# Routed attention and a gated feed-forward on one core: values of four steps behind one pair of score steps

## Chip, cores and metric

The kernel runs on one core of one Trainium2 chip. The metric is the device time of one execution in microseconds (us). A core has a matrix engine (TensorE, PE in the profile), VectorE (DVE), ScalarE (ACT), GpSimd (POOL) and a queue engine for transfers (SyncE, SP). They run beside each other and wait for one another by semaphores. Each works through its own instructions in the order in which the program gives them, so the order of the program on each engine is a thing that one can tune. This kernel fixes that order by hand.

## What is computed

```python
# q, k, v: (4, 8, 768, 64); centroids: (8, 16, 64); w_in: (512, 2048); w_out: (2048, 512)
q_assign = argmax(einsum('bhsd,hcd->bhsc', q_n, c_n))      # the nearest of 16 centroids of the head
k_assign = argmax(einsum('bhsd,hcd->bhsc', k_n, c_n))
mask = q_assign[:, :, :, None] == k_assign[:, :, None, :]
scores = where(mask, q @ k.T / 8, -1e9)
attn = softmax(scores)
x = (attn @ v) with heads joined                            # (3072, 512)
h = x @ w_in
out = (h * clip(h + 3, 0, 6) / 6) @ w_out                   # (3072, 512)
```

## The kernel before

Two heads make a *pair*; there are 16 pairs. Each pair has two halves of queries (384 columns) and six chunks of keys, so 12 *steps*, 192 in all. A step is: scores of a chunk of keys with half the queries for both heads (`ps`), the mask as a second product with one-hot rows (`xm`) added in PSUM, the exponential on ScalarE (`ex`), the sum over keys on GpSimd (`acc`), and the values (`pv`), which gather over six steps in one PSUM bank. Per half pair `divide` sums `acc` over partitions with a product by ones (`pd`), takes the reciprocal and scales.

```python
def scores(n):
    g, hf, j = where(n)                  # pair, half, chunk of keys
    if ("ps", n) not in st:
        scores_qk(n)                     # 2 matmuls, one for each head: 64 rows of the array each
    scores_part(n, st["xm", g], False)   # 2 more, bf16: the mask
    sc = st.pop(("ps", n))[:, :, 0:HALF]
    ex = expp.tile([P, 2, HALF], F32, name="ex")          # expp has 4 buffers, psum_s has 2
    nc.scalar.activation(out=ex, in_=sc, func=ACT.Exp, scale=SM_SCALE)
    ...
    nc.gpsimd.tensor_tensor(out=acc, in0=acc, in1=ex, op=ALU.add)

def attn_v(n):
    if j == 0:
        st["pv"] = psum_v.tile([P, 512], F32, name="pv")  # psum_v has 1 buffer
    for t in range(2):                                     # one head each: 64 columns of the array
        nc.tensor.matmul(pv[t * D : (t + 1) * D], lhsT=vt[:, j, t], rhs=ex[:, t],
                         start=(j == 0), stop=(j == NCH - 1))
    if j == NCH - 1:
        nc.scalar.copy(out=num, in_=pv)
```

The feed-forward is cut into 12 blocks of 256 tokens. From the second block on its products are done with seven half-size products in place of eight. A block has eight "up" items and seven "down" items. An up item makes four groups of gates, in two PSUM banks (X, then Y, of two that rotate); VectorE adds them up, ScalarE makes the lift and VectorE the clip, and each two items GpSimd makes further sums of the gates.

```python
def halved(b, m, u, i, g):
    part(X[:, 0], ...); part(X[:, 1], ...); part(X[:, 2], ...)      # uX: 12 matmuls in the trace
    nc.vector.tensor_copy(out=sx[:, 1], in_=X[:, 1])
    add(sx[:, 0], X[:, 0], sx[:, 1]); add(sx[:, 2], X[:, 2], sx[:, 0])
    finish()                                                        # clip of the item before
    part(Y[:, 0], ...); ...; part(Y[:, 3], ...)                     # uY: 16
    add(sx[:, 3], Y[:, 0], sx[:, 0]); add(g[:, 3], Y[:, 0], sx[:, 2])
    add(g[:, 0:3], Y[:, 1:4], sx[:, 1:4])
    lift(sx, g)                                                     # ScalarE
    ending.append(lambda: (clip(g, sx, g), gated_sums(i)))          # what finish() runs
```

In the second block each up item also makes four differences of `w_in` on VectorE (`first_sums`), which later blocks load back.

The main loop goes by *double steps*. Items fill the time in which the attention waits:

```python
for n in range(0, total + lag_d + 2, 2):
    for i in (n, n + 1):
        scores(i)                        # with its exponential and key sum
    for i in (n - 2, n - 1):
        attn_v(i)
    m = n - 3
    if m % NCH == NCH - 1:
        later.append(divide(m))
    prep = prep_items(g + 1, r)          # turning q and k, centroid scores, one-hot rows of the next pair
    ...
    want = items_by(n + 2) - done        # items of the feed-forward; interleaved with prep
    ...
    decode steps of the weights          # in the first half of the pairs alone (n < 96)
    checks                               # copies and accumulations that guard the ranges (ScalarE)
```

Of the kernel before, what the change touches and what calls it, by code (L numbers as in the profile page):

```python
# [8 lines left out]
F32 = mybir.dt.float32  # L9
# [107 lines left out]
def fast_path(ctx, tc, ok, q, k, v, centroids, moe_w_in, moe_w_out, out):  # L117
# [11 lines left out]
    vp = pool("vp", 2)  # L129
    xp = pool("xp", 2)  # L130
    rtp = pool("rtp", 1)
    smallp = pool("smallp", 1)
    expp = pool("expp", 4)
    accp = pool("accp", 2)
    nump = pool("nump", 1)
    xnp = pool("xnp", 2)
# [5 lines left out]
    decoding = ctx.enter_context(ExitStack())  # L142
    rawp = decoding.enter_context(tc.tile_pool(name="rawp", bufs=2))
    decp = decoding.enter_context(tc.tile_pool(name="decp", bufs=2))
    psum_s = pool("psum_s", 2, space=PSUM)
    psum_v = pool("psum_v", 1, space=PSUM)
    psum_t = pool("psum_t", 1, space=PSUM)
# [16 lines left out]
    counts = const.tile([P, 2, NPAIR], F32, name="counts")  # L164
    w_low = const.tile([P, 1], F32, name="w_low")

    st = {}
    later = []

    def scratch(shape, name, dtype=F32):  # L170

# [81 lines left out]

    cen = const.tile([P, D], F32, name="cen")
    parity = const.tile([P, 2], F32, name="parity")

    def constants():
        make_identity(nc, ident)  # L260
        for t in range(2):
            nc.vector.tensor_reduce(
                out=parity[:, t : t + 1],
                in_=ident.rearrange("p (h t c) -> p t h c", t=2, c=C)[:, t], axis=AX.XY, op=ALU.max,
            )
        nc.gpsimd.memset(half_c, 0.5)
        nc.gpsimd.memset(low_c, 1.0 / BOUND)
        nc.gpsimd.memset(ones, 1.0)
        nc.gpsimd.memset(w_low, W_LOW)
        nc.gpsimd.memset(one_hot, 0.0)  # L270

        warm = psum_t.tile([P, 4, P], F32, name="warm", tag="t")
        for i in range(14):
            nc.tensor.transpose(out=warm[:, i % 4], in_=ident, identity=ident)

    def centroid_norm():
        cn = unit_rows(nc, smallp, cen, D)

        nc.scalar.activation(out=w_totals[:, 0, 0:1], in_=w_low, func=ACT.Exp)

        wide = smallp.tile([P, 2, D], F32, name="cenwide")
        for t in range(2):
            nc.vector.tensor_scalar_mul(out=wide[:, t], in0=cn, scalar1=parity[:, t : t + 1])
        st["wide"] = wide
# [37 lines left out]
    def route(g):  # L322
        cs = st.pop(("cs", g))
        pr = scratch([P, NC2, 2, C], "pr")
        for i in range(NC2 // 4):
            nc.tensor.transpose(out=pr[:, 4 * i : 4 * i + 4], in_=cs[:, i], identity=ident)
        pr = pr.rearrange("p j t c -> p (j t) c")
        mx = rtp.tile([P, 2 * NC2], F32, name="mx")
        nc.vector.reduce_max(out=mx, in_=pr, axis=AX.X)
        oh = one_hot.rearrange("p j (t c) -> p j t c", t=2)[:, :, :, 0:C]  # L330
        pr = pr.rearrange("p (j t) c -> p j t c", t=2)
        mx = mx.rearrange("p (j t) -> p j t", t=2)
        halves = [slice(0, NCH), slice(NCH, NC2)]
# [14 lines left out]

        later.append(count)

    def route_turn(g, part):
# [7 lines left out]
        nc.scalar.activation(out=dst, in_=po, func=ACT.Copy, scale=-FAR if part else 1.0)  # L359


    def where(n):
# [8 lines left out]
    def scores_part(n, x, first):  # L371
        g, hf, j = where(n)
        for t in range(2):
            r = slice(t * D, (t + 1) * D)
            nc.tensor.matmul(  # L375
                st["ps", n][:, t, 0:HALF], lhsT=x[r, NCH + j],
                rhs=x[r, hf * NHC : (hf + 1) * NHC], start=first, stop=not first,
            )

    def scores(n):  # L380
        g, hf, j = where(n)
        if ("ps", n) not in st:
            scores_qk(n)
        scores_part(n, st["xm", g], False)
        sc = st.pop(("ps", n))[:, :, 0:HALF]
        ex = expp.tile([P, 2, HALF], F32, name="ex")
        nc.scalar.activation(out=ex, in_=sc, func=ACT.Exp, scale=SM_SCALE)  # L387
        st["ex", n] = ex
# [140 lines left out]
    def ffn_items(b):  # L529
# [47 lines left out]
        def halved(b, m, u, i, g):  # L577
# [25 lines left out]
            nc.vector.tensor_copy(out=sx[:, 1], in_=X[:, 1])  # L603
            add(sx[:, 0], X[:, 0], sx[:, 1])
            add(sx[:, 2], X[:, 2], sx[:, 0])
            finish()
            Y = psum_m.tile([P, 4, P], F32, name="uY", tag="m")
            part(Y[:, 0], tx[:, 0], s(0))
            part(Y[:, 1], wi(1, 0, i), a(1, 0))
# [3 lines left out]
            add(g[:, 3], Y[:, 0], sx[:, 2])  # L613
            add(g[:, 0:3], Y[:, 1:4], sx[:, 1:4])
            lift(sx, g)
            ending.append(lambda: (clip(g, sx, g), gated_sums(i)))

        def product(bank, half, kind, w, first, last, again, chunks=range(HF)):
# [58 lines left out]

    def prep_items(g, r):  # L680

        if g >= NPAIR:
            return []
        return {
            0: [lambda: turn(g, 0), lambda: turn(g, 1)],
            2: [lambda: turn(g, 2)],
            4: [lambda: cluster_scores(g)],
            6: [lambda: route(g)],
            8: [lambda: route_turn(g, 0)],
            10: [lambda: route_turn(g, 1)],  # L690
        }.get(r, [])

    per_pair = 2 * NCH
# [17 lines left out]
        return up_first + (n - DECODED) * (per_ffn + 11) // per_batch  # L711

    st["early"] = st["free"] = True
    fill, checks = [], []
    done = 0

    with tc.manual_schedule():
        nc.scalar.dma_start(cen, centroids.rearrange("h c d -> (h c) d"))
        load(0, "q", "k")
        constants()  # L720
        load(0, "v")
        load_weights(0)
        centroid_norm()
        for part in range(3):
            turn(0, part)
        centroid_turn()
        nc.vector.tensor_copy(out=ident_q, in_=ident)
        load(1, "q", "k")
        cluster_scores(0)
        scores_qk(0)  # L730
        route(0)
        scores_qk(1)
        for part in range(2):
            route_turn(0, part)

        for n in range(0, total + lag_d + 2, 2):
            g, r = divmod(n, per_pair)
            for i in (n, n + 1):
                if i < total:
                    scores(i)  # L740
            for i in (n - lag_v, n - lag_v + 1):
                if 0 <= i < total:
                    attn_v(i)
            m = n - lag_d + 1
            if m >= 0 and m % NCH == NCH - 1:
                later.append(divide(m))
            prep = prep_items(g + 1, r)
            if r == 4 and prep:
                prep.pop()()
            if n == DECODED:  # L750
                st["early"] = False
            if m >= 0 and m % per_batch == per_batch - 1:
                fill += ffn_items(m // per_batch)
            if r == 6:
                load(g + 2, "q", "k")
                load(g + 1, "v")
            want = items_by(n + 2) - done
            want = min(want, len(fill))
            done += want
            for i in range(max(len(prep), want)):  # L760
                if i < want:
                    fill.pop(0)()
                if i < len(prep):
                    prep[i]()
            for step in decode[: share[r]]:
                step()
            del decode[: share[r]]
            for check in checks:
                check()
            checks, later[:] = later[:], []  # L770

        while checks:
            for check in checks:
                check()
            checks, later[:] = later[:], []
        for item in fill:
            item()

# [384 lines left out]
```

## Time and profile before

| what | value |
|---|---|
| time, median of 3 runs | 1046.78 us (1046.28 to 1048.92) |
| span of the profiled run | 1048.3 us, granted TensorE clock 0.994 |
| PE busy | 1013.2 us (97%) |
| DVE, ACT, POOL busy | 587.8, 387.5, 406.4 us |
| scores of pair 8 begin, last values end | about 251 and 828 us |

The page has busy times of each engine over the span, then the span in 40 slices, then the chain that ended last, then groups of instructions with the idle time before them and who ended it. Busy time of one engine over the whole span is an average over stages: here attention with decoding of weights (to about 250 us), attention with items of the feed-forward (to about 828 us), items alone. A matmul in the trace carries the form of the array that it uses, rows*columns: 64*128 for scores, 128*64 for values, 128*128 for the rest. Float32 matmuls appear twice each in the trace (one instruction is two rows), so a step's two products of values are four rows.

### The profile page before, as it was taken

The numbers are of one execution on the slowest core, as the hardware profiler recorded it, in microseconds if no ns is written. First come the engines' busy times: TensorE is split into PE (matmuls) and PEld (weight loads), VectorE is DVE, ScalarE is ACT, GpSimd is POOL, SyncE is SP. The second block draws the span as 40 slices with busy tenths as digits, with TensorE's granted clock in tenths as the row PEclk, the third lists the DMA queues.
The fourth block names the chain that finished last, engine by engine and source line by source line (L and its number), as shares of the span: only waits on it lengthen the run. The fifth ranks groups of instructions, "written<-read, shape, count | busy, mean of one in ns | idle before, by whom it ended". The sixth has DMA issues, their size and how long they took to land.

```text
span 1048.3 us, 16637 instructions
## 1 busy us (share of the span) xinstructions
PE 1013.2 (97%) x6560; PEld 740.9 (71%) x6560; DVE 587.8 (56%) x1117; ACT 387.5 (37%) x764; POOL 406.4 (39%) x315
## 2 busy tenths in 40 slices
PE   8999989999998999999999999999999999999996
PEld 4444445546767778677777777777778798989995
DVE  4899987868477247246246345345245373727270
ACT  6888866674223233223223233233223111102010
POOL 3777657664234235135234235235334220303030
PEclk9999999999999999999999999999999999999999
DMA  6455554531043223223322232333032051414120
GB/s 164 107 141 142 161 143 111 141 84 46 31 118 104 54 81 89 53 66 84 73 71 88 64 89 64 71 94 96 3 91 86 1 144 34 142 42 140 51 61 25
DMA packets 107176, 90.34 MB, mean 86 GB/s; under 512 B 78416, under 2 KB 88656, under 8 KB 107088
## 3 DMA queue, kind: packets, MB, share of 16 engines
q1 hardware_dynamic: 106944, 89.15, 31.2%
q8 instruction: 54, 0.88, 0.3%
q14 instruction: 34, 0.28, 0.1%
q10 hardware_dynamic: 144, 0.03, 0.0%
HBM read 73.43 MB, written 15.73 MB: 85 GB/s over the span
## 4 chain that ended last, share of the span: by engine, by line
PE 76%; DVE 8%; ACT 2%; issue 1%; DMA 1%; SPq 1%; DVEq 0%; ACTq 0%
PE Y L620 16%; PE uY L585 13%; PE X L620 12%; PE ps L375 10%; PE uX L585 10%; PE pv L404 9%; PE ph L540 3%; DVE rcp L429 2%; PE pd L425 1%; DVE sx L596 1%; PE pqk L302 1%; DVE num L430 1%; DVE g_sb L456 1%; PE pcs L315 1%; SPq L191 1%
## 5 line engine op out<-in xcount | busy, mean ns | idle before, releaser
L394 POOL TENSOR_TENSOR acc<-acc,ex 128x768 f32<-128x768 f32 x128 | 239.6, 1872 | 226.8 <-ACT ex L387 220.9
L575 POOL TENSOR_TENSOR g_sb<-g_sb 128x256 f32<-128x256 f32 x144 | 105.9, 756 | 219.2 <-DVE g_sb L456 216.4
L453 ACT ACTIVATE sx<-g_sb,half_c 128x512 f32<-128x512 f32 x88 | 63.5, 722 | 304.7 <-DVE g_sb L596 304.7
L387 ACT ACTIVATE ex<-ps 128x768 f32<-128x768 f32 x192 | 146.4, 803 | 75.4 <-PE ps L375 75.1
L375 PE MATMUL ps<-xf 64*128 64x384 f32 x768 | 165.5, 509 | 4.0 <-ACT ex L387 4.0
L404 PE MATMUL pv<-ex,vt 128*64 128x384 f32 x768 | 145.1, 499 | 0.0
L391 POOL TENSOR_TENSOR acc<-ex 128x768 f32<-128x768 f32 x32 | 59.0, 1842 | 161.9 <-ACT ex L387 161.9
L429 DVE RECIPROCAL rcp<-pd 128x384 f32<-128x384 f32 x32 | 81.8, 2555 | 57.8 <-PE pd L425 57.8
L627 DVE TENSOR_TENSOR y<-y,Y 128x256 f32<-128x256 f32 x48 | 20.2, 420 | 157.8 <-PE Y L620 157.0
L404 PEld LDWEIGHTS pv<-ex,vt 128*64 128x64 f32 x768 | 46.6, 136 | 80.1 <-issue 75.8
L375 PEld LDWEIGHTS ps<-xf 64*128 64x128 f32 x768 | 63.1, 186 | 46.1 <-issue 28.8
L585 PE MATMUL uX<-xb,w_in_sb 128*128 128x128 f32 x704 | 93.8, 277 | 0.0
L620 PE MATMUL X<-w_out_sb,g_sb 128*128 128x256 f32 x384 | 91.4, 387 | 0.4 <-DVE sx L596 0.4
L620 PE MATMUL Y<-T,g_sb 128*128 128x256 f32 x384 | 87.6, 381 | 0.0
L620 PE MATMUL Y<-w_out_sb,g_sb 128*128 128x256 f32 x384 | 87.5, 381 | 0.0
L585 PEld LDWEIGHTS uX<-xb,w_in_sb 128*128 128x128 f32 x704 | 86.5, 194 | 0.0
L620 PEld LDWEIGHTS X<-w_out_sb,g_sb 128*128 128x128 f32 x384 | 71.9, 192 | 16.3 <-issue 6.1
L456 DVE SCALAR_TENSOR_TENSOR g_sb<-sx,g_sb 128x512 f32<-128x512 f32 x88 | 76.8, 873 | 8.8 <-ACT sx L453 8.8
L620 PEld LDWEIGHTS Y<-T,g_sb 128*128 128x128 f32 x384 | 72.0, 190 | 13.5 <-issue 4.2
L620 PEld LDWEIGHTS Y<-w_out_sb,g_sb 128*128 128x128 f32 x384 | 72.2, 190 | 13.0 <-issue 3.6
L603 DVE COPY sx<-uX 128x128 f32<-128x128 f32 x88 | 25.5, 290 | 84.5 <-PE uX L585 84.5
L375 PE MATMUL ps<-xm 64*128 64x384 bf16 x384 | 63.1, 323 | 3.1 <-ACT xm L359 2.8
(109 smaller groups left out, 1448.4 us busy)
## 6 DMA issues: line engine op xcount, KB each, us to landing
tx<-td SPq DMA_DIRECT2D x80, 384.0 KB, 3.2
raw<-in_moe_w_in_dram SPq DMA_DIRECT2D x16, 512.0 KB, 3.9
raw<-in_moe_w_out_dram SPq DMA_DIRECT2D x16, 512.0 KB, 3.7
qk<-in_q_dram SPq DMA_DIRECT2D x32, 192.0 KB, 4.6
qk<-in_k_dram SPq DMA_DIRECT2D x32, 192.0 KB, 4.8
vt<-in_v_dram SPq DMA_DIRECT2D x32, 192.0 KB, 4.4
xd<-num SPq DMA_DIRECT2D x32, 192.0 KB, 3.9
xb<-xd SPq DMA_DIRECT2D x12, 512.0 KB, 4.4
```

The lines of the kernel that those rows point to most:

```text
L375: nc.tensor.matmul(st["ps", n][:, t, 0:HALF], lhsT=x[r, NCH + j], rhs=x[r, hf * NHC : (hf + 1) * NHC], start=first, stop=not first,)
L387: nc.scalar.activation(out=ex, in_=sc, func=ACT.Exp, scale=SM_SCALE)
L391: nc.gpsimd.tensor_tensor(out=acc, in0=st["ex", n - 1], in1=ex, op=ALU.add)
L394: nc.gpsimd.tensor_tensor(out=acc, in0=acc, in1=ex, op=ALU.add)
L404: nc.tensor.matmul(pv[t * D : (t + 1) * D], lhsT=vt[:, j, t], rhs=ex[:, t], start=(j == 0), stop=(j == NCH - 1),)
L429: nc.vector.reciprocal(out=rcp, in_=pd)
L453: nc.scalar.activation(out=r, in_=h, func=ACT.Relu, bias=half_c, scale=1.0 / 6.0)
L456: nc.vector.scalar_tensor_tensor(out=g, in0=r, scalar=1.0, in1=h, op0=ALU.min, op1=ALU.mult)
L540: nc.tensor.matmul(ph[:, t * HC : (t + 1) * HC], lhsT=w_in_sb[:, kt, f * P : (f + 1) * P], rhs=st["xb", b, m][:, kt], start=(kt == 0), sto ...
L575: eng.tensor_tensor(out=out_, in0=in0, in1=in1, op=op)
L585: nc.tensor.matmul(dst, lhsT=w[:, kt], rhs=x(kt), start=(kt == 0), stop=(kt == HK - 1))
L620: nc.tensor.matmul(bank[:, half * HC : (half + 1) * HC], lhsT=g_sb[:, kind, i], rhs=w[:, i], start=(first and i == 0), stop=(last and i == ...
```

## The change

In the second half of the pairs (n of 96 and more) the loop goes by four steps. A double step with r = 0, 4, 8 does its scores, and then the values of all steps up to n, which are four; it has no items. A double step with r = 2, 6, 10 does its scores and then the items of both. Key sums and the divisions move with them: the first half of a pair is divided at r = 8, in the middle of the values, the second at r = 4 of the next pair ahead of them. At r = 8 the values cross from one half pair to the next, and the second exponential stands behind them. Six `ex` buffers hold what values wait for. In `halved` the clip of the item before (`finish`) stands behind the Y sums and the lift instead of between the X sums and Y. Preparation of the next pair is gathered at r = 2, 6 and 10. The aim is fewer alternations between kinds of matmul, and sums that are not held up by a clip.

The text also holds another way of masking on VectorE (`masks`, `clusters`, `spread`), for pairs from number `MASKED` on. `MASKED` is 16 and pairs are 0 to 15, so it is never run; what is left of it are 16 small memsets at the start. The centroid tiles go to a pool that ends with the decoding of weights.

```diff
-    expp = pool("expp", 4)
+    expp = pool("expp", 6)
...
+    MASKED = NPAIR
...
+        for c in range(C):
+            nc.gpsimd.memset(number[:, c : c + 1], float(c))
...
             add(sx[:, 2], X[:, 2], sx[:, 0])
-            finish()
             Y = psum_m.tile([P, 4, P], F32, name="uY", tag="m")
...
             lift(sx, g)
+            finish()
             ending.append(lambda: (clip(g, sx, g), gated_sums(i)))
...
+        if fours:
+            return {2: turns, 6: scores_of + ways, 10: one_hots}.get(r, [])
...
+    def four_by_four(n, r, steps):
+        for i in steps:
+            scores(i)
+        if r % 4 == 2:
+            for i in steps:
+                exponentials(i)
+            unmasked.extend(steps)
+            check_all()
...
+            return
+        for i in steps[: 1 if r == 8 else 2]:
+            exponentials(i)
+        check_all()
+        for i in unmasked:
+            masks(i)
+            key_sums(i)
+        unmasked.clear()
+        if r == 4 or n >= total:
+            m = n - r % per_pair - 1 if n < total else total - 1
+            if ("acc", *where(m)[:2]) in st and m < st["valued"]:
+                later.append(divide(m))
+                ready(m)
+        for i in range(st["valued"], min(n, total)):
+            attn_v(i)
+            if i % per_pair == NCH - 1:
+                later.append(divide(i))
+        st["valued"] = min(n, total)
+        for i in steps[1 if r == 8 else 2 :]:
+            exponentials(i)
+        for i in steps:
+            masks(i)
+            key_sums(i)
...
+            fours = n >= DECODED
...
+            if fours:
+                four_by_four(n, r, steps)
+            else:
...
-            want = items_by(n + 2) - done
...
+            if not fours or r % 4 == 2 or n >= total:
+                want = min(items_by(n + 2) - st["done"], len(fill))
```

More of the change, by code (lines that the diff above doesn't have):

```diff
@@ L131, in fast_path @@
     rtp = pool("rtp", 1)
+    kidp = pool("kidp", 2)
     smallp = pool("smallp", 1)
-    expp = pool("expp", 4)
+    expp = pool("expp", 6)
     accp = pool("accp", 2)
@@ L144, in fast_path @@
     decp = decoding.enter_context(tc.tile_pool(name="decp", bufs=2))
+    startp = decoding.enter_context(tc.tile_pool(name="startp", bufs=1))
     psum_s = pool("psum_s", 2, space=PSUM)
@@ L165, in fast_path @@
     w_low = const.tile([P, 1], F32, name="w_low")
+    MASKED = NPAIR
     st = {}
     later = []
+    numbers = []
     def scratch(shape, name, dtype=F32):
@@ L252, in decoding_steps @@
         return [split, join, power, rest, total]
-    cen = const.tile([P, D], F32, name="cen")
+    cen = startp.tile([P, D], F32, name="cen")
     parity = const.tile([P, 2], F32, name="parity")
+    number = const.tile([P, C], BF16, name="number")
     def constants():
@@ L276, in centroid_norm @@
     def centroid_norm():
-        cn = unit_rows(nc, smallp, cen, D)
+        cn = unit_rows(nc, startp, cen, D)
         nc.scalar.activation(out=w_totals[:, 0, 0:1], in_=w_low, func=ACT.Exp)
-        wide = smallp.tile([P, 2, D], F32, name="cenwide")
+        wide = startp.tile([P, 2, D], F32, name="cenwide")
         for t in range(2):
@@ L349, in route @@
         later.append(count)
+        if g >= MASKED:
+            numbers.append(lambda: clusters(g))
     def route_turn(g, part):
@@ L359, in route_turn, with by_vector, clusters, spread @@
         nc.scalar.activation(out=dst, in_=po, func=ACT.Copy, scale=-FAR if part else 1.0)
+    def by_vector(n):
+        return where(n)[0] >= MASKED
+    def clusters(g):
+        oh = one_hot.rearrange("p j (t c) -> p j t c", t=2)[:, :, :, 0:C]
+        which = rtp.tile([P, NC2, 2, C], BF16, name="which")
+        nc.vector.tensor_tensor(
+            out=which, in0=oh, in1=number.unsqueeze(1).unsqueeze(1).to_broadcast([P, NC2, 2, C]), op=ALU.mult
+        )
+        qid = st["qid"] = rtp.tile([P, NCH, 2], BF16, name="qid")
+        kid = st["kid", g] = kidp.tile([P, NCH, 2], F32, name="kid")
+        nc.vector.tensor_reduce(out=kid, in_=which[:, NCH:], axis=AX.X, op=ALU.add)
+        nc.vector.tensor_scalar(
+            out=kid, in0=kid, scalar1=-1.0, scalar2=C * (C - 1) / 2.0, op0=ALU.mult, op1=ALU.add
+        )
+        qsum = rtp.tile([P, NCH, 2], F32, name="qsum")
+        nc.vector.tensor_reduce(out=qsum, in_=which[:, 0:NCH], axis=AX.X, op=ALU.add)
+        nc.vector.tensor_copy(out=qid, in_=qsum)
+    def spread(g, part):
+        if part == 0:
+            st["xm", g] = xp.tile([P, NC2, P], BF16, name="xm")
+        pb = scratch([P, 4, P], "pb")
+        for i in range(4):
+            t, j = divmod(4 * part + i, NCH)
+            nc.tensor.matmul(
+                pb[:, i], lhsT=st["qid"][:, j, t : t + 1].to_broadcast([P, P]), rhs=ident_q,
+                start=True, stop=True,
+            )
+        nc.scalar.copy(out=st["xm", g][:, 4 * part : 4 * part + 4], in_=pb)
     def where(n):
@@ L376, in scores_part, with exponentials, masks, key_sums @@
                 st["ps", n][:, t, 0:HALF], lhsT=x[r, NCH + j],
-                rhs=x[r, hf * NHC : (hf + 1) * NHC], start=first, stop=not first,
+                rhs=x[r, hf * NHC : (hf + 1) * NHC], start=first,
+                stop=not first or by_vector(n),
             )
     def scores(n):
-        g, hf, j = where(n)
         if ("ps", n) not in st:
             scores_qk(n)
-        scores_part(n, st["xm", g], False)
+        if not by_vector(n):
+            scores_part(n, st["xm", where(n)[0]], False)
+    def exponentials(n):
         sc = st.pop(("ps", n))[:, :, 0:HALF]
-        ex = expp.tile([P, 2, HALF], F32, name="ex")
+        ex = st["ex", n] = expp.tile([P, 2, HALF], F32, name="ex")
         nc.scalar.activation(out=ex, in_=sc, func=ACT.Exp, scale=SM_SCALE)
-        st["ex", n] = ex
+    def masks(n):
+        g, hf, j = where(n)
+        if not by_vector(n):
+            return
+        ex = st["ex", n]
+        for t in range(2):
+            nc.vector.scalar_tensor_tensor(
+                out=ex[:, t].rearrange("p (a b) -> p a b", b=P),
+                in0=st["xm", g][:, t * NCH + hf * NHC : t * NCH + (hf + 1) * NHC],
+                scalar=st["kid", g][:, j, t : t + 1], in1=ex[:, t].rearrange("p (a b) -> p a b", b=P),
+                op0=ALU.is_equal, op1=ALU.mult,
+            )
+    def key_sums(n):
+        g, hf, j = where(n)
+        ex = st["ex", n]
         if j == 1:
@@ L673, in ffn_items, with prep_items @@
         return items
-    def prep_items(g, r):
+    def prep_items(g, r, fours):
         if g >= NPAIR:
             return []
-        return {
[L685 to L690, printed above, removed]
+        turns = [lambda part=part: turn(g, part) for part in range(3)]
+        one_hots = [lambda: route_turn(g, 0), lambda: route_turn(g, 1)]
+        if g >= MASKED:
+            one_hots = [lambda part=part: spread(g, part) for part in range(3)]
+        scores_of = [lambda: cluster_scores(g)]
+        ways = [lambda: route(g)]
+        if fours:
+            return {2: turns, 6: scores_of + ways, 10: one_hots}.get(r, [])
+        return {
+            0: turns[:2], 2: turns[2:], 4: scores_of, 6: ways, 8: one_hots[:1], 10: one_hots[1:],
         }.get(r, [])
@@ L713, in fast_path, with check_all, ready @@
     st["early"] = st["free"] = True
-    fill, checks = [], []
-    done = 0
+    fill, checks, unmasked = [], [], []
+    st["done"], st["valued"] = 0, DECODED - lag_v
+    def check_all():
+        now, checks[:] = checks[:], []
+        for check in now:
+            check()
+    def ready(m):
+        if m % per_batch == per_batch - 1:
+            fill.extend(ffn_items(m // per_batch))
+    def four_by_four(n, r, steps):
[6 more added lines that the diff above has]
+            check_all()
+            for op in numbers:
+                op()
+            numbers.clear()
+            return
+        for i in steps[: 1 if r == 8 else 2]:
[20 more added lines that the diff above has]
+            key_sums(i)
     with tc.manual_schedule():
@@ L737, in fast_path @@
             g, r = divmod(n, per_pair)
-            for i in (n, n + 1):
-                if i < total:
-                    scores(i)
[L741 to L749, printed above, removed]
+            fours = n >= DECODED
+            steps = [i for i in (n, n + 1) if i < total]
+            prep = prep_items(g + 1, r, fours)
+            if fours:
+                four_by_four(n, r, steps)
+            else:
+                for i in steps:
+                    scores(i)
+                    exponentials(i)
+                    key_sums(i)
+                for i in (n - lag_v, n - lag_v + 1):
+                    if i >= 0:
+                        attn_v(i)
+                m = n - lag_d + 1
+                if m >= 0 and m % NCH == NCH - 1:
+                    later.append(divide(m))
+                    ready(m)
+            if prep and r == (6 if fours else 4):
+                prep.pop(0)()
             if n == DECODED:
                 st["early"] = False
-            if m >= 0 and m % per_batch == per_batch - 1:
-                fill += ffn_items(m // per_batch)
             if r == 6:
@@ L756, in fast_path @@
                 load(g + 1, "v")
-            want = items_by(n + 2) - done
[L758 to L764, printed above, removed]
+            if not fours or r % 4 == 2 or n >= total:
+                want = min(items_by(n + 2) - st["done"], len(fill))
+                st["done"] += want
+                for i in range(max(len(prep), want)):
+                    if i < want:
+                        fill.pop(0)()
+                    if i < len(prep):
+                        prep[i]()
             for step in decode[: share[r]]:
@@ L767, in fast_path @@
             del decode[: share[r]]
-            for check in checks:
-                check()
-            checks, later[:] = later[:], []
+            if not fours:
+                for op in numbers:
+                    op()
+                numbers.clear()
+                check_all()
+            checks.extend(later)
+            later.clear()
         while checks:
-            for check in checks:
-                check()
-            checks, later[:] = later[:], []
+            check_all()
+            checks.extend(later)
+            later.clear()
         for item in fill:
```

## Prediction

> **What bounds the kernel now.** I read the page from the top: busy time by engine, then the 40 slices, then the chain that ended last. Each column of the slices is 26 us, and a digit is the busy share in tenths.
>
> ```profile
> PE 1013.2 (97%) x6560; PEld 740.9 (71%) x6560; DVE 587.8 (56%) x1117; ACT 387.5 (37%) x764; POOL 406.4 (39%) x315
> PE   8999989999998999999999999999999999999996
> ...
> PEclk9999999999999999999999999999999999999999
> ...
> PE 76%; DVE 8%; ACT 2%; issue 1%; DMA 1%; SPq 1%; DVEq 0%; ACTq 0%
> ```
>
> TensorE (PE) is busy for 97% of the span at full clock, and the chain runs through it. The half that is changed begins where the scores of pair 8 begin, at 251 us, and ends with the last values at about 828 us; after that only items are left. The view of windows divides it:
>
> ```profile
> 0.00:252.00 252.00, 237.63 (x1474) 0.99 0.49 126
> 252.00:330.00 78.00, 73.19 (x469) 0.98 0.24 76
> 330.00:860.00 530.00, 522.76 (x3439) 1.00 0.27 74
> 860.00:1040.00 180.00, 179.61 (x1182) 1.00 0.25 72
> ```
>
> The columns are the stretch, its length, PE busy with its matmuls, granted clock, DMA share, GB/s. From 252 us on 12.4 us of PE are not busy, so waits cannot be where much is won. But "busy" also counts slow starts of matmuls. So I read the timeline of PE in one double step (start, busy, operation; two steps of scores `ps`, values `pv`, then an item, `uX`/`uY`):
>
> ```profile
> 622.83 0.61 PE L585 MATMUL uY<-xb,tx 128*128 128x128 f32 x4
> 623.27 0.61 PE L585 MATMUL uY<-xs,w_in_sb 128*128 128x128 f32 x4
> 623.82 0.92 PE L375 MATMUL ps<-xf 64*128 64x384 f32 x4
> 624.57 0.33 PE L375 MATMUL ps<-xm 64*128 64x384 bf16 x2
> 624.73 0.81 PE L375 MATMUL ps<-xf 64*128 64x384 f32 x4
> 625.37 0.33 PE L375 MATMUL ps<-xm 64*128 64x384 bf16 x2
> 625.63 1.51 PE L404 MATMUL pv<-ex,vt 128*64 128x384 f32 x8
> 627.07 0.71 PE L585 MATMUL uX<-xs,tx 128*128 128x128 f32 x4
> 627.62 1.06 PE L585 MATMUL uX<-xb,w_in_sb 128*128 128x128 f32 x8
> ```
>
> The form behind the operation is rows*columns of the array: 64*128 for scores, 128*64 for values, 128*128 for all else. Compare start with start. Four uY matmuls inside a run take 0.44 us (622.83 to 623.27), the last four before scores 0.55: 0.11 lost. The first score group takes 0.75 (623.82 to 624.57), the second 0.64: 0.11 lost. From `xm` to scores is 0.16, from `xm` to values 0.26: 0.10 lost. The first uX group takes 0.55 against 0.44 in a run: 0.11. The eight values take 1.44 from their first start to the next engine form; four pairs 0.32 us apart would be 1.28, so 0.16 more. That makes 0.11 + 0.11 + 0.10 + 0.16 + 0.11 = 0.59 us per double step, spent on three changes of form and on nothing else. Over 48 double steps that is 28 us: this is what the change goes after.
>
> **What the Trainium skill says.** "TensorEngine Tiling (Array Packing)", Tiling Modes, Key Properties: changing the tiling mode, not just the tile, drains the engine. The trace agrees: every change of form costs about 0.1 us at the seam, and po to uX, both 128*128, costs nothing. No figure for it stands there; the 0.1 us is the trace's. "Perfetto Trace Analysis", Tensor Engine Instruction: the start of a matmul is recorded, its end is computed. Hence I use starts alone; the overlapping spans above (623.27 + 0.61 is later than 623.82) show why. "SBUF — State Buffer", SBUF: two separate sides: a GpSimd operation and a VectorE operation with two SBUF inputs exclude each other for a whole instruction. The trace agrees: the clip (L456), which has two, takes 0.68 us alone and 1.12 or 1.20 where GpSimd's additions run beside it.
>
> **The change part by part.**
>
> 1. *Order of scores and values.* Per four steps PE ran scores, values, items twice: six changes of form, 2 x 0.59 = 1.18 us. It now runs scores, values of four steps, scores, items: four changes. Two of these are known: items to scores 0.22, scores to values 0.10 + 0.05 (the slow first pair, the part of the 0.16 that is not at the seam after values). Values to scores and scores to items occur nowhere in this trace; I estimate each from its neighbours as one seam plus one slow first group, 0.10 + 0.11 = 0.21. Sum 0.22 + 0.15 + 2 x 0.21 = 0.79. Saved 1.18 - 0.79 = 0.39 by rounded starts; with 0.54 instead of 0.59 per double step (unrounded starts) it is 1.08 - 0.74 = 0.34. I take 0.35 x 24 groups of four = 8.4 us, less 0.4 for the end, where the last values stand alone between items: **-8.0 us**. All of it is on the path, since PE is the path.
>
> 2. *Values at r = 8 cross the middle of a pair.* Steps 4 and 5 end one accumulation, 6 and 7 begin the next in the one `pv` bank, so step 6 waits for the copy of `num` on ScalarE (0.48 us). Before, a whole item lay between. What covers it: `pd`, two matmuls, 0.65 us. With an idle ScalarE the copy would be ready as `pd` ends. But ScalarE first does one exponential (0.8 us) and the two counts with their accumulator reads, 2 x (0.36 + 0.19) = 1.1 us; where the last item was an "up" its lift (0.72) comes before that. From the start of the scores: lift ends 2.1, exponential 2.9, counts 4.0, copy 4.5, plus about 0.2 to PE, against 3.9 when `pd` ends. So about 0.8 us lost where an up precedes, nearly nothing where a down does; for eight pairs **+1.5 us** (about 2 in full, the rest in part).
>
> 3. *Scores of the second double step* need the banks that the first two exponentials free. Values last 2.7 us, exponentials end 1.7 us after the scores, even behind a lift 3.5 us after their start against 4.5. **0**.
>
> 4. *Items come four or five in a row.* For each up, VectorE has 0.29 + 2 x 0.29 before and 0.29 + 0.28 + 0.55 after the uY end, and a clip of 0.68 to 1.2: with gaps 2.9 us against 3.13 of PE. It just fits, as it does in the tail of the kernel before, where eight ups stand in a row and the window 860:1040 has only 0.4 us idle. The exception is the second block (292 to 330 us), where each up also makes four weight sums (about 1.75 us): VectorE needs 4.6. Before, PE waited there 1.6, 0.6 and 2.4 us in runs of two. Now five of its eight ups stand in one run: I reckon four waits of 1.0 to 1.5. Against that one attention phase of 6.5 us in place of two of 3.3. **+0.5 us**.
>
> 5. *The clip behind the next sums.* Before, clip i stood between the uX sums and the uY sums of item i+1, and a clip of 1.2 us made the uY sums late (uY starts of 0.48 to 0.52 instead of 0.45). Now it is after them, and the next uX sums are late instead: uY ends, sums 1.25, clip 0.7 to 1.2, uX sums 0.97, so the bank is free after 2.9 to 3.4 us, and PE wants it after 3.13. One small wait for another. At a block's end the extra clip runs while the last lift (0.72) is awaited. **0**, at most 1 us either way.
>
> 6. *The rest.* `masks`, `clusters` and `spread` are never reached: the bound is pair 16 and there are 16 pairs, 0 to 15. What stays of them is 16 memsets of 0.1 us on GpSimd before it idles from 2.8 to 17.4 us: **0**. Two more `ex` buffers let values wait four steps: needed, not a gain.
>
> Sum: -8.0 + 1.5 + 0.5 = -6.0, so 1046.8 - 6.0 = 1040.8. The estimate for values to scores may be a little high, and bursts leave VectorE freer elsewhere; I settle on **1040.5 us**, 0.6% faster.
>
> **Rivals.**
>
> *A new wait eats it all.* Bursts of items with VectorE at 2.9 of 3.13 us, key sums bunched into four (4 x 1.82 = 7.3 us of GpSimd in a row) that lengthen each clip and sum, and `num` on the path. For: the 0.5 us of margin per item is thin, and the clip did reach 2.19 us once. Against: the tail runs eight ups in a row without loss. It would make 1046 to 1050.
>
> *The seams are bound to the number of groups, not to modes.* If values to scores cost far more (0.4 us, a full drain with weights that cannot be loaded ahead in either half form), the saving falls to 0.15 x 24 = 3.6 us: 1045.
>
> *The gain is larger.* If values to scores and scores to items cost only the seam, 0.1 each, the saving is 0.6 x 24 = 14 us, 1035 with the waits. For: weight loads of one form may run ahead. Against: every first group seen after a change was slow.
>
> **Range and chances.** From the rivals: 1035 at the favourable end, 1046 at the other. 2% is 21 us, which the 28 us of seams cannot give when four of six stay, and no wait found comes near +21. Faster by over 2%: 0.02; within: 0.96; slower: 0.02.
>
> **What would show it.** In the timeline: per four steps one run of 16 values of about 2.7 us (not 2 x 1.44), and seams of 0.1 us with slow first groups at values to scores and scores to items. In the waits: a row of PE waiting for ScalarE's `num` of about 0.2 to 0.8 us, up to eight times; sums on `uX` from VectorE in the 300 to 330 us stretch of about the same total. Idle time of PE from 252 us on should stay under 16 us. The prediction is wrong if PE waits for exponentials after values, if uX waits spread over all blocks, or if PE's busy time falls by much more or less than 8 us.

## The result and the profile after

The changed kernel takes 1041.9 us (median of four runs, 1038.4 to 1042.8) against 1047.55 us: a ratio of 0.994, 95% interval 0.9913 to 0.9967. In a later measurement on another occasion it was 0.996 (0.9943 to 0.9977). The prediction was 1040.5 us in a range of 1035 to 1046.

The total came out nearly as predicted. Its parts did not. The timeline of PE in the changed kernel, items, scores, values of four steps, scores, items:

```profile
323.87 0.61 PE L648 MATMUL uY<-xs,w_in_sb 128*128 128x128 f32 x4
324.41 0.92 PE L419 MATMUL ps<-xf 64*128 64x384 f32 x4
...
325.97 0.33 PE L419 MATMUL ps<-xm 64*128 64x384 bf16 x2
326.23 2.80 PE L467 MATMUL pv<-ex,vt 128*64 128x384 f32 x16
328.96 0.92 PE L419 MATMUL ps<-xf 64*128 64x384 f32 x4
329.71 0.33 PE L419 MATMUL ps<-xm 64*128 64x384 bf16 x2
...
330.52 0.33 PE L419 MATMUL ps<-xm 64*128 64x384 bf16 x2
330.77 0.71 PE L648 MATMUL uX<-xs,tx 128*128 128x128 f32 x4
331.32 0.94 PE L648 MATMUL uX<-xb,w_in_sb 128*128 128x128 f32 x7
```

Sixteen values take 2.73 us from first start to the next form (326.23 to 328.96), where two runs of eight took 2 x 1.44. The two changes of form that the old trace did not contain cost what was estimated: the first scores after values take 0.75 (328.96 to 329.71), not 0.64; scores to items take 0.25 (330.52 to 330.77) where 0.16 is the step to a matmul of the same form; and the first uX group takes 0.55, not 0.44.

What PE waits for, from the start of pair 8 on (who waits for whom: us in total, times, longest; rows of 0.4 us and less are left out). First the kernel before, then the changed one:

```profile
PE uX L585 <- DVE sx L596: 7.9, 9, 2.4
PE pqk L302 <- DVE rcp L429: 2.0, 1, 2.0
PE uY L585 <- DVE g_sb L596: 1.7, 4, 0.6
```

```profile
PE pcs L323 <- DVE rcp L492: 8.9, 2, 7.1
PE uX L648 <- DVE sx L659: 6.2, 5, 1.9
```

The waits for sums (`uX`, `uY`) fell by 3.4 us, and a wait that I had not named, the one for the reciprocal `rcp`, rose from 2.0 to 8.9 us. Before, it held up the turning of q and k (`pqk`), now the centroid scores `pcs`: both, like `pd`, use the one scratch bank of PSUM in this half (`psum_t` has 1 buffer). One of its two places lost 7.1 us. Here are VectorE and then PE at that place (start, busy, operation):

```profile
559.88 1.98 DVE L519 SCALAR_TENSOR_TENSOR g_sb<-sx,g_sb 128x512 f32<-128x512 f32 x1 [0.25 <-ACT sx L516]
561.90 7.75 DVE L638 TENSOR_TENSOR g_sb<-g_sb 128x256 f32<-128x256 f32 x4
569.57 2.54 DVE L492 RECIPROCAL rcp<-pd 128x384 f32<-128x384 f32 x1
```

```profile
564.72 0.33 PE L419 MATMUL ps<-xm 64*128 64x384 bf16 x2
572.17 1.50 PE L323 MATMUL pcs<-xf,cnT 128*32 128x384 f32 x8 [7.12 <-DVE rcp L492]
```

And GpSimd beside them:

```profile
559.00 8.42 POOL L457 TENSOR_TENSOR acc<-acc,ex 128x768 f32<-128x768 f32 x4
567.39 1.98 POOL L454 TENSOR_TENSOR acc<-ex 128x768 f32<-128x768 f32 x1
```

The four gate sums that end a block take 1.56 us on VectorE where GpSimd is idle, as in the kernel before:

```profile
918.91 1.56 DVE L575 TENSOR_TENSOR g_sb<-g_sb 128x256 f32<-128x256 f32 x4
```

Here they take 7.75, about four times the 1.9 us of one key sum: taken one by one, they start 0.1 to 0.5 us behind a key sum each (561.90, 563.85, 565.69, 567.63 against 561.39, 563.61, 565.56, 567.39). GpSimd has five key sums in a row: the four of two double steps, which are now issued together, and the first of the next. The reciprocal waits behind the gate sums, it alone frees the bank of `pd`, and `pcs`, straight behind the scores of r = 6, wants that bank.

**A tally of starts.** To compare kernels I add up, over all matmuls from the first scores of pair 8 to the last one, the time from one start to the next. Each kind has a fixed spacing inside a run (0.112 us for uX and uY, 0.216 for X and Y, 0.323 for a pair of values, and so on); what is left over is sorted. *Seams* are changes of form with the slow first group after them. *Rest* is waits, and matmuls at half clock: the granted clock of a trace drops to 0.5 for stretches of 3.41 us, or two of them together, and matmuls in them start at about twice the spacing. The last column says about how much of the rest that is. The fixed spacings sum to 738.2 us in every kernel of this study.

| kernel | ratio to before (95%) | first scores of pair 8 to last matmul | seams | rest | of rest: bank wanted by `pcs` | of rest: half clock |
|---|---|---|---|---|---|---|
| before | 1 | 788.4 | 27.3 | 23.0 | 0 | 3.0 |
| changed | 0.994 (0.9913 to 0.9967) | 782.9 | 18.9 | 25.9 | 9.0 | 3.9 |
| clip moved only | 1.0029 (1.0015 to 1.0043) | 789.0 | 27.3 | 23.6 | 0 | 1.6 |
| order only | 0.9892 (0.9867 to 0.9917) | 776.7 | 18.9 | 19.5 | 5.7 | 2.9 |
| key sums at once | 0.9875 (0.9851 to 0.9899) | 773.1 | 18.9 | 15.9 | 2.8 | 1.5 |
| centroid scores later | 0.9868 (0.9844 to 0.9891) | 773.8 | 20.4 | 15.4 | 0 | 3.3 |
| last sums on GpSimd | 0.9846 (0.9826 to 0.9866) | 772.1 | 19.0 | 15.1 | 0 | 1.6 |
| three mends | 0.9878 (0.9856 to 0.990) | 775.7 | 20.4 | 17.3 | 0 | 0 |
| values each double step | 0.9857 (0.9834 to 0.9879) | 771.8 | 24.0 | 9.8 | 0 | 0 |
| last sums on GpSimd, clip back | 0.9816 (0.9793 to 0.9839) | 768.0 | 19.0 | 11.0 | 0 | 0 |
| last sums on GpSimd, key sums at once | 0.9841 (0.9819 to 0.9864) | 770.9 | 19.0 | 13.8 | 0 | 1.6 |
| last sums on GpSimd, values each | 0.9848 (0.9821 to 0.9874) | 770.5 | 22.6 | 9.9 | 0 | 0 |
| before, last sums on GpSimd | 0.9964 (0.9952 to 0.9976) | 784.4 | 27.3 | 19.1 | 0 | 1.4 |

The stretch ahead of pair 8 differs by up to 6 us between single executions of the same instructions (with the new order it ends at 244.8 to 250.6 us in these traces), so the tally, which leaves it out, is sharper than one span: a second trace of the changed kernel gives 783.0. But each row is one trace, and a half-clock stretch, about 1.6 us, can stand in one trace and be missing in the next (last section). Differences of the rest are sound only beyond that.

### The profile page after: what moved, and what is told of

It is laid out like the page before. It is cut to its first block, busy times and chain, and to the rows that moved or that the text cites. A ratio compares the mean times of both kernels' runs of the same rounds, so it can differ in the third digit from the quotient of the medians.

```text
span 1041.0 us, 16706 instructions
## 1 busy us (share of the span) xinstructions
PE 1005.3 (97%) x6560; PEld 742.6 (71%) x6560; DVE 600.4 (58%) x1117; ACT 389.6 (37%) x764; POOL 411.0 (39%) x331
## 4 chain that ended last, share of the span: by engine, by line
PE 85%; DVE 5%; ACT 5%; DMA 3%; issue 1%; SPq 1%; ACTq 0%; DVEq 0%
PE Y L683 16%; PE uY L648 14%; PE ps L419 13%; PE X L683 12%; PE uX L648 11%; PE pv L467 10%; PE ph L603 3%; PE pqk L310 2%; PE pd L488 2%; PE pcs L323 1%; ACT ex L434 1%; DVE g_sb L638 1%; DVE g_sb L519 1%; ACT xm L369 1%; DMA raw<-in_moe_w_in_dram 1%
## 5 line engine op out<-in xcount | busy, mean ns | idle before, releaser
L457 POOL TENSOR_TENSOR acc<-acc,ex 128x768 f32<-128x768 f32 x128 | 244.8, 1912 | 207.2 <-ACT ex L434 201.4
L467 PE MATMUL pv<-ex,vt 128*64 128x384 f32 x768 | 141.1, 496 | 0.0
L467 PEld LDWEIGHTS pv<-ex,vt 128*64 128x64 f32 x768 | 48.7, 136 | 78.2 <-issue 70.0
```

## Experiments

**Clip moved only.** On the kernel before:

```diff
             add(sx[:, 2], X[:, 2], sx[:, 0])
-            finish()
...
             lift(sx, g)
+            finish()
```

> The kernel before with the clip moved behind the next sums and nothing else. My theory (the clip is worth nothing, one small wait for another): within 1.5 us of the kernel before, so 1046 to 1049, seams and order of scores and values unchanged, PE's waits for VectorE at uX and uY together between 8 and 12 us as before (7.9 + 1.7). Rival (the clip is where the gain comes from): 3 us or more faster.

Measured: 1049.2 us, ratio 1.0029 (1.0015 to 1.0043), so slower. In the tally the rest is 0.6 us more: the slow uY starts behind uX went from 3.5 us to 0.1, and uX waits grew instead, one wait for another as was expected. But the interval of the ratio means 1.6 to 4.5 us, which is more than 0.6 and more than the 1.5 us that my theory allowed. The half clock hides the rest: the trace of the kernel before has two such stretches (3.0 us), this one has one (1.6). Without them the rest rises from 20.0 to 22.0 us, and these 2.0 us lie within the interval. Both expectations failed: the clip behind the sums is a small loss.

**Order only.** The changed kernel with these two lines put back.

> The changed kernel with the clip put back between the uX and uY sums, so the order of scores, values and items alone. My theory (the order carries the gain, 8 us of seams saved less about 3 us of new waits): 1041 to 1043, PE busy 7 to 9 us under the kernel before. Rival (the clip is what makes runs of items cheap): 1045 or more, with more uX and uY waits for VectorE.

Measured: 1034.25 us, ratio 0.9892. Both theories failed: without the moved clip the change is worth about twice as much (1.1% against 0.4 to 0.6%). The rest is 19.5 us instead of 25.9. Of the 6.4 us, 3.3 are the bank's wait (5.7 instead of 9.0) and 2.7 the waits from uY to uX (3.4 instead of 6.1). The waits of its PE:

```profile
PE pcs L323 <- DVE rcp L492: 5.6, 1, 5.6
PE uX L648 <- DVE sx L659: 3.7, 4, 1.7
```

**Key sums at once.** The changed kernel, without the collecting:

```diff
-            unmasked.extend(steps)
+            for i in steps:
+                key_sums(i)
```

> The changed kernel, key sums of the r = 2, 6, 10 steps issued at once and not kept until the next double step, so that GpSimd has two in a row instead of four. Theory of the lock (a block's last gate sums on VectorE alternate one by one with GpSimd's row of key sums, the reciprocal stands behind them, and the bank it reads is wanted by the centroid scores): the wait of the centroid scores for the reciprocal falls from 8.9 us to under 4, and the time by 3 to 6 us to 1036 to 1039. Rival (VectorE is late for another reason, the row of key sums does not matter): wait of 7 to 10 us stays, 1041 to 1043.

Measured: 1032.4 us, ratio 0.9875; the bank's wait 2.7 us in one place. The row of key sums is a part of the cause, as the theory has it. The gain is larger than expected: of the 10.0 us by which the rest fell, 6.2 are the bank's wait and about 2.4 the half clock.

**Centroid scores later.**

```diff
-            return {2: turns, 6: scores_of + ways, 10: one_hots}.get(r, [])
+            return {2: turns, 6: [lambda: None] + scores_of + ways, 10: one_hots}.get(r, [])
...
-            if prep and r == (6 if fours else 4):
+            if prep and r == 4 and not fours:
```

> The changed kernel, centroid scores at r = 6 behind two items instead of straight behind the scores. The sums on VectorE stay as slow as they were, but nothing on PE wants the bank for 7 us. If the wait for the bank is the loss: no wait of the centroid scores for the reciprocal over 1 us, PE busy as in the changed kernel, 1033 to 1036. Rival (the wait only moves to the next thing that needs VectorE, the gate sums of the first item or the one-hot rows): waits of PE for VectorE come up elsewhere by 5 us or more, 1040 to 1043.

Measured: 1032.55 us, ratio 0.9868. No wait for the reciprocal is left, and none came up elsewhere. The gate sums stayed slow (33.9 us busy in 48, as in the changed kernel), so their slowness alone shows no cost in this trace: what cost was that PE wanted the bank behind them. The seams rose by 1.5 us, because `pcs` between items changes form twice.

**Last gate sums on GpSimd.**

```diff
-            eng = nc.vector if i == HF - 1 else nc.gpsimd
+            eng = nc.gpsimd
```

> The changed kernel, the gate sums of a block's last item on GpSimd like all the others, so that VectorE has no four sums with two SBUF inputs to push through GpSimd's row of key sums. Theory of the lock: at the place where these four sums took 7.75 us, VectorE goes straight to the reciprocal, the wait of the centroid scores for it is under 1.5 us in place of 8.9; the sums now come behind the key sums on GpSimd, so PE may wait about 1 us for them in a down item; 1033 to 1038. Rival (VectorE is late by its own backlog, GpSimd has no part): the wait stays at 6 us or more, 1040 to 1043.

Measured: 1028.8 us, ratio 0.9846. The same place, VectorE:

```profile
554.14 0.69 DVE L519 SCALAR_TENSOR_TENSOR g_sb<-sx,g_sb 128x512 f32<-128x512 f32 x1 [0.25 <-ACT sx L516]
554.96 2.56 DVE L492 RECIPROCAL rcp<-pd 128x384 f32<-128x384 f32 x1
```

and GpSimd:

```profile
554.91 2.90 POOL L638 TENSOR_TENSOR g_sb<-g_sb 128x256 f32<-128x256 f32 x4 [1.61 <-DVE g_sb L519]
557.77 7.79 POOL L457 TENSOR_TENSOR acc<-acc,ex 128x768 f32<-128x768 f32 x4
```

The four sums take 2.90 us on GpSimd, ahead of the key sums and not behind them as I had written, and the clip takes 0.69 in place of 1.98. The reciprocal follows the clip. That VectorE's sums and GpSimd's held each other up, and were not late by VectorE's own backlog, is shown by this run together with the one on key sums at once.

**The changed kernel again.**

> The changed kernel once more beside the others on one chip: 1040 to 1043, and its trace shows whether the wait of the centroid scores for the reciprocal (8.9 us in two places) comes again in the same places. If it does, it belongs to the order of instructions; if it is in other places or gone, it is chance.

Measured: 1040.6 us. Its trace has the wait in the same two places, 8.9 us, longest 7.1. It belongs to the order of instructions, not to chance.

**Three mends together**: clip back, key sums at once, centroid scores later.

> The changed kernel with three mends: clip back between the sums, key sums of r = 2, 6, 10 at once, centroid scores behind two items. If the gains of the three are separate losses taken away (in their traces from the start of pair 8 to the end 6.2, 9.6 and 9.1 us against the changed kernel, but the first two and the third all remove the same wait): no wait for the reciprocal, seams as in the changed kernel (about 19 to 20 us), waits and slow matmuls about 11 to 13 us instead of 25.9; 1028 to 1031. If the clip does nothing once the wait for the bank is gone: as the two alone, 1032.

Measured: 1032.5 us, ratio 0.9878: a miss. The three do not add up. The time is the rival's 1032, but the two other mends without the clip were not tried, so the rival's reason is not shown. Slow uY starts came back with 6.1 us, eight waits for gate additions (3.8 us) among them. With key sums at once they run under the first items of a row, and a clip that stands between the sums takes 2 us beside one. In the trace of this kernel, GpSimd, VectorE and PE:

```profile
474.47 1.81 POOL L457 TENSOR_TENSOR acc<-acc,ex 128x768 f32<-128x768 f32 x1
474.77 2.07 DVE L519 SCALAR_TENSOR_TENSOR g_sb<-sx,g_sb 128x512 f32<-128x512 f32 x1
477.84 0.68 PE L648 MATMUL uY<-xs,tx 128*128 128x128 f32 x4 [0.41 <-DVE g_sb L659]
```

My reading is that the place of the clip has two prices: between the sums it is bad where key sums run under items, behind them it is bad where VectorE is already late. No run here moves the clip alone with key sums at once, so the first half of that is not shown.

**Values each double step**, on the three mends; the division of the first half moves to the head of r = 8:

```diff
         if r % 4 == 2:
             ...
+            for i in range(st["valued"], min(n, total)):
+                attn_v(i)
+            st["valued"] = min(n, total)
             return
...
+        if r == 8:
+            later.append(divide(n - 3))
         for i in range(st["valued"], min(n, total)):
             attn_v(i)
-            if i % per_pair == NCH - 1:
-                later.append(divide(i))
```

> The kernel with the three mends, but values of two steps behind every double step's scores, while items stay gathered per four steps: five changes of form per four steps in place of four. Theory of the seams: by my sums 0.88 us per four steps against 0.74, so 0.14 times 24 = 3.5 us slower than its twin. Rival (what saves time is that items stand in a long row, whatever stands between): the same as its twin within 1 us.

Measured: 1030.7 us, ratio 0.9857. The seams are 24.0 us against 20.4, 3.6 more, as the sum has it (3.5). The forecast of a slower total failed all the same: the median is 1.8 us lower, with intervals that overlap, and the tally 3.9 us shorter, because the rest fell from 17.3 to 9.8, with no half clock in either trace: the slow uY starts are gone (1.0 instead of 6.1 us). Two more values between scores and items let key sums get ahead of the clips; that reason is argued from the order, it was not tried alone.

**On top of the sums on GpSimd: clip back; key sums at once; values each double step.**

> The changed kernel, last gate sums on GpSimd and the clip back between the uX and uY sums. It asks what the clip's place is worth once nothing waits for the bank. From the order-only trace, waits and slow matmuls without those of the bank are 13.2 us, from the kernel with sums on GpSimd and a late clip 15.1: so about 2 us faster than that one, 1026 to 1028. Rival (the late clip harmed only by making the last gate sums later): the same as that one within 1 us, 1028 to 1030.

Measured: 1026.1 us, ratio 0.9816, the fastest kernel here and 1.8% faster than before. The rest is 11.0 us instead of 15.1: late uX starts fell from 6.1 to 3.4 us, and 1.6 us are a half-clock stretch that this trace does not have. So the late clip cost about 2.5 us even where nothing waits for the bank, as in the old order (2.0).

> The changed kernel, last gate sums on GpSimd and key sums at once, clip late. If long rows of GpSimd also stretch clips and sums elsewhere: 1 to 3 us below the kernel with the gate sums on GpSimd alone, 1026 to 1028. If the block's last sums were the only place where the row mattered: the same, 1028 to 1030.

Measured: 1028.5 us, ratio 0.9841, against 0.9846 without: the same within their intervals; by the tally 1.2 us less.

> Values of two steps behind every double step's scores, items of both gathered, key sums at once, clip between the sums, last gate sums on GpSimd, centroid scores straight behind the values. Seams and slow first groups 23 us (3.5 us more than the changed kernel, about 1 less than the kernel with values each double step, whose centroid scores stood between items), waits 10: from the start of pair 8 to the end about 776, 1025 to 1028. If centroid scores at their old place bring the wait for the bank back: 1029 or more.

Measured: 1029.0 us, ratio 0.9848, no wait for the bank. That is 1 us above what I forecast, and not for the reason that the rival gave. The nearest kernel is the fastest one, which also has the clip back; against it both the values and the key sums are changed. The seams are 3.6 us more (22.6 against 19.0), the rest 1.1 less, the tally 2.5 longer. Here the seams decide, though the 1.1 cannot be split between the two edits.

**The kernel before with the last sums on GpSimd.**

> The kernel before with the last gate sums of each block on GpSimd, nothing else. If the exclusion of VectorE's sums and GpSimd is a loss of the new order alone: 1 to 3 us faster than the kernel before (it has one wait of 2.0 us of the turns of q and k for the reciprocal), 1043 to 1046. Rival (these sums cost 8 to 12 us in the old order too, hidden in other waits): 1038 or less.

Measured: 1042.1 us, ratio 0.9964, so 2.5 to 5.0 us faster: more than the 1 to 3 of my theory, far from the rival's 8 to 12. It takes away the one old wait for the reciprocal and the slow matmuls behind it, 3.9 us of rest. With the last sums on VectorE the rest was 3.9 us larger in the old order and 10.8 us (25.9 against 15.1) in the new one.

## Why the prediction was right, step by step

*Step 1, the seams, held.* Predicted 8.0 us less, measured 8.4 (27.3 to 18.9). Both estimated seams had the size of their neighbours. The rivals on their size are out, and the two kernels with values each double step show the same price from the other side, 3.6 us for 24 changes. One reading of mine is off: `po` to uX is not free. The first four uX behind it take 0.50 us (617.38 to 617.88 in the kernel before) against 0.44 in a run. Both orders have that. And the last values of the kernel before end at about 839 us, not 828: those of the last two steps stand behind one more item (837.67 to 839.12).

*Step 2, the copy of `num`, held in size, not in its places.* +1.5 us was predicted. The table of waits has no row for it in the changed kernel, because the computed end of `pd` lies later than the next start. The starts show it (`pd`, the copy on ScalarE, the next values):

```profile
374.19 0.81 PE L488 MATMUL pd<-acc,ones 128*64 128x384 f32 x4
374.41 0.48 ACT L473 COPY num<-pv 128x384 f32<-128x384 f32 x1
374.94 1.51 PE L467 MATMUL pv<-ex,vt 128*64 128x384 f32 x8
```

At all eight crossings the values start 0.05 us after the copy ends, 0.75 us after `pd` starts in place of 0.65, and their first pair is 0.05 us slow: 0.15 us each, 1.2 us in all. I had expected about 0.8 us where an up precedes and nearly nothing elsewhere; ScalarE's other work delayed the copy nowhere. That the sum agrees is partly luck.

*Step 3, no wait for exponentials after values, held*: there is no such row from pair 8 on.

*Step 4, items in a row, failed twice, in opposite directions.* In the second block the three late starts are 1.7, 0.7 and 2.0 us (4.4) against 5.1 before: 0.7 less, not 0.5 more. Outside it I saw no gain to be had, and there was one. In the old order a division stood right before an item, so VectorE's sums of the uX products waited behind the reciprocal. VectorE in the kernel before:

```profile
381.14 2.56 DVE L429 RECIPROCAL rcp<-pd 128x384 f32<-128x384 f32 x1 [3.03 <-PE pd L425]
...
384.26 0.28 DVE L603 COPY sx<-uX 128x128 f32<-128x128 f32 x1
```

Here PE's next uX started 0.74 us late. There are six such places between 385 and 715 us (at one of them a down item is late), by 0.5 to 0.74 us each, 3.5 us in all. In the new order the reciprocal runs under values and scores, and those late starts are gone.

*The missing step.* Nowhere did I ask who wants the bank of `pd` next. I left out the gate sums at a block's end (1.56 us alone), although I had shown the lengthened clip as a sign that VectorE and GpSimd exclude each other, and I rejected the rival of the bunched key sums by the tail of the kernel, where eight ups run without loss. The tail has no key sums. This rival was the right mechanism at a place it did not name: +9.0 us, and 2.3 more at half clock behind it. The totals that I had named as signs could not show that: PE's busy time fell by 7.9 us and its idle time from 252 us on was 15.5, both as predicted. The rows of the waits showed it.

*Step 5, the clip, failed.* 0, at most 1 us, was predicted. With the half clock left out, the tally has 2.0 us in the old order, about 2.5 in the new one where nothing waits for the bank, and about 5.4 where the bank's wait grows with it (order only against changed). The argument that the uX bank is free after 2.9 to 3.4 us took VectorE to be on time. Where it is behind, in the second block and behind the last reciprocal, a clip ahead of the next uX sums is paid in full.

Summed by the tally: -8.4 seams, +2.9 rest, -5.5; predicted -6.0. The rest is +9.0 for the bank, +1.2 for `num` and -7.3 net for all other waits and slow matmuls. Of the +2.0 that the prediction had for waits, only the 1.5 for `num` has a counterpart. The right total is part luck: two unseen terms of opposite sign.

## What to carry to other kernels

When the order of one engine is changed, list for every shared single buffer who frees it and who wants it next in the *new* order; PE waited 7 us for a bank that a 2.5 us reciprocal held, because four small sums stood ahead of it. Here additions with two SBUF operands on VectorE and on GpSimd shut each other out, so bunching one engine's row multiplies the other's time (1.56 to 7.75 us); put small sums where the other engine's row is not, or on the same engine. And count changes of array form: at 0.10 us for the seam and 0.05 to 0.11 for the slow first group they can be summed from a trace before anything is changed.

## What the runs showed of the hardware beyond that

A wait of PE can be paid twice. Behind the wait of 1.98 us in the kernel before, the granted clock was 0.5 for 3.41 us, and eight matmuls that span 1.73 us from first start to next start elsewhere took 3.03. The windows view (stretch, length, PE busy, clock, DMA share, GB/s) and the timeline have:

```profile
422.80 0.66 PE L302 MATMUL pqk<-ident,qk 128*128 128x128 f32 x4 [1.98 <-DVE rcp L429]
423.67:427.08 3.41, 3.41 (x10) 0.50 0.68 174
```

The length of the wait alone does not decide it. In the kernel with the clip moved only, a wait of 3.09 us had no such sequel: the eight uX matmuls behind these four take 0.90 us from first start to the next group, 0.89 in a run.

```profile
326.22 0.71 PE L585 MATMUL uX<-xs,tx 128*128 128x128 f32 x4 [3.09 <-DVE sx L596]
```

From pair 8 on, no wait of up to 1.83 us in any trace of this study was followed by half clock, waits of 1.84 to 1.89 us were in 6 of 12 cases, and all longer ones but that of 3.09. "TensorE: Matmul & The Clock Gate" in the Trainium skill (What's actually happening) has a throttle that is the default and that activity releases, in windows of about 3.4 us that run freely. The length of the slow stretches agrees. The page lets the throttle come back after at least one idle window; here waits of 1.84 to 2.74 us, shorter than that, were enough. That the place of a wait in the free-running windows decides would fit, but no run here shows it. In the changed kernel the wait of 7.1 us had 6.83 us at half clock, which cost 2.3 us on top; with both waits for the bank gone (last sums on GpSimd) the rest fell by 10.8.
